# Two heads' scores on the two row halves of the array: three half-height passes in place of two full-height ones, in a fused attention, expert and feed-forward kernel

## The chip, the cores and the metric

One Trainium2 chip, one core. The metric is the time of one execution on the device in microseconds (us). PE is the matrix engine (TensorE), PEld its weight loads, DVE the vector engine, ACT the scalar engine, POOL GpSimd, SP the queue that issues most DMAs. PSUM is the memory into which PE writes; its pools here take it in banks.

## The reference

The program computes three stages one after another. Only the first matters for most of the change.

```
B, H, S, D = 2, 8, 768, 64                   # attention: 4 sink keys, a window of 128
scores = (q @ k.T) / sqrt(D); keep = (key < n_sink) | (0 <= row - key < window)
a = softmax(where(keep, scores, -1e9)); x = a @ v          # x becomes 1536 rows of 512
# experts: 8 of 512 -> 1024 -> 512 with relu, one for each row
logits = normalised(x) @ normalised(expert_emb).T / tau
y[row] = softmax(logits)[best] * relu(x[row] @ w1[best]) @ w2[best]
# feed-forward: 512 -> 2048 -> 512
out = leaky(y @ w_in) @ w_out
```

## The kernel before

**Attention.** Query rows are taken in blocks of 128, heads in groups of four. A step of the loop in `attention` is one block of one head: there are 2 batches x 2 groups x 6 blocks x 4 heads = 96 steps. At each step `score` makes one head's scores of a block against the keys that its window and the sinks can reach (256 or 288 columns). Some steps later `flip` turns the exponentials on PE, and `value` multiplies them with v (tiles `tp` and `xp`, lines L299, L317, L320). Beside these run, for the next group, the turning of q and k from rows to columns (`turns`, L206), and for each finished block of rows the router: its turn (L729) and its product with the expert embeddings (`lg`, L749).

**Two parts of each number.** Scores are products of numbers cast to `fp32r`. What the cast drops is kept too: q and k are held in a high part (the cast, written by ACT, L212 and L226) and a low part (the rest, written by DVE, L217 and L229). A head has 64 dimensions. Before, the tile `head_k` holds the high part of k on one half of the 128 partitions and the low part on the other, and `head_q` holds q's high part on both halves, and its low part on both. So one product over 128 rows gives q_high x (k_high + k_low), a second gives q_low x (k_high + k_low). For q to land on both halves it is copied on POOL before it is turned (L172), and each head's q is turned by itself. So a pair of heads takes 3 turns for k and 6 for q for each half of the rows.

**Order.** In the attention, a scheduler that simulates the engines sets the order of instructions on each engine; from the experts on, PE's order is that of the code. Each engine works through its own queue in order. Tiles in PSUM come from pools: `ps_sc` (scores, three banks, also the small router results `lg`, `rk`, `cnt`), `ps_t` (turned tiles, four banks), `ps_x` (one). A product into a tile waits until the earlier user of its buffer has been read. `stir` and `fill` are products whose results nobody reads.

**Behind the attention.** `rank_experts` and `route` find out on DVE which rows go to which expert, while PE works on one unit of a guessed expert (L1338, L1356). Then come the eight experts (`moe_wide`, `moe_narrow`, `moe_whole`) and the feed-forward part (`ffn`). Some weights are split into high and low parts in between (`Work.pop`, L1157 and L1158). `pick` checks that no score was out of the range in which the shortcut holds.

Of the kernel before, what the change touches and what calls it, by code (L numbers as in the profile page):

```python
# [57 lines left out]
TURNS = {(0, 0): ([0, 1, 2], [3, 4, 5, 6, 7, 8]), (0, 1): ([11, 13, 15, 17, 19, 21], [25, 26, 27, 28, 29, 30]),  # L58
         (1, 0): ([33, 35, 37, 39, 41, 43], [56, 57, 59, 60, 61, 62]), (1, 1): ([47, 49, 50, 51, 53, 54], [67, 69, 71, 73, 75, 77])}
# [89 lines left out]
def attention(c, ctx):  # L149
# [14 lines left out]
    def load_qk(b, pr, c0=0, n=QB):  # L164
        rk, rq = raws[b, pr] = c.raws[pr % 2]
        for j in range(2):
            nc.sync.dma_start(out=rk[:, c0:c0 + n, j, :],
                              in_=c.k[b, 2 * pr + j].rearrange("(c p) d -> p c d", p=P)[:, c0:c0 + n])
        for j in range(2):
            nc.sync.dma_start(out=rq[:, c0:c0 + n, j, 0, :],  # L170
                              in_=c.q[b, 2 * pr + j].rearrange("(c p) d -> p c d", p=P)[:, c0:c0 + n])
            c.copied = nc.gpsimd.tensor_copy(rq[:, c0:c0 + n, j, 1, :], rq[:, c0:c0 + n, j, 0, :])  # L172
# [22 lines left out]
    def turns(b, pr):  # L195

        rk, rq = raws[b, pr]
        own = slice(0, D), slice(D, P)  # L200
        two = [c.heads[(b * H + 2 * pr + j) % 8] for j in range(2)]
# [22 lines left out]
        def q_part(c0, j):  # L224
            t, w, qt = turn(rq[:, :, j], c0, f"q{j}"), slice(c0 * P, (c0 + 3) * P), two[j][1]
            nc.scalar.activation(out=qt[:, 0, w], in_=t, func=AF.Copy, scale=-0.125)  # L226

            def rest():
                c.low_half = nc.vector.scalar_tensor_tensor(out=qt[:, 1, w], in0=t, scalar=-0.125, in1=qt[:, 0, w].bitcast(F32),  # L229
                                                            op0=ALU.mult, op1=ALU.subtract)  # L230

            later(step[0] >= 0, rest)

        for j in range(2):
            heads[b, 2 * pr + j] = two[j]
        return [[lambda c0=c0, o=o: k_part(c0, o)] + [lambda c0=c0, j=j: q_part(c0, j) for j in range(2)]
                for c0, o in ((0, 0), (3, BEHIND))]

# [7 lines left out]
    copied = c.copied  # L246
# [18 lines left out]
    def score(b, g, i, h):  # L265
# [5 lines left out]
        off, n, m, _, s0 = SPAN[i]  # L271
        kt, qt = heads[b, 4 * g + h]
# [8 lines left out]
        c.scored = nc.vector.tensor_tensor_reduce(out=p, in0=sc[:, 0:n], in1=m, scale=1.0, scalar=3.0e38,  # L281
# [94 lines left out]
    for m in (2, 0, 2):  # L376
        turn[0, 0][0].pop(0)()
        stir(m)
    s = 0
    while s < n or after:  # L380
# [5 lines left out]
        if s < n:  # L386
# [17 lines left out]
            if s == 1:  # L404
                with tc.issue_after(copied.ins):
                    c.others()
# [13 lines left out]
def pick(c, T, over):  # L420
# [4 lines left out]
    part, big, ok = T([P, 1], "part"), T([P, 1], "big"), T([P, 4], "ok")  # L425
    nc.vector.tensor_reduce(out=part, in_=c.los, axis=AX.X, op=ALU.max)
# [315 lines left out]
def router_logits(c, t, pool=None):  # L742
# [3 lines left out]
    lp = (pool or c.psc).tile([P, E], F32, tag="sc", name=f"lg{c.uid()}")  # L746
    with c.tc.issue_after(turned.ins):
        for kk in range(4):
            c.logged = nc.tensor.matmul(lp, lhsT=xT[:, kk, :], rhs=c.embT[:, kk, :], start=(kk == 0), stop=(kk == 3))  # L749
    lg, top, idx, oh = c.lg[:, t, :], c.top[:, t], c.idx[:, t:t + 1], c.oh[:, t, :]  # L750
    nc.vector.tensor_scalar(out=lg, in0=lp, scalar1=0.0, scalar2=None, op0=ALU.add, op1=ALU.max, accum_out=top)
# [8 lines left out]
def router_rank(c, t0, t1, pool=None):  # L760
# [3 lines left out]
    rk = (pool or c.psc).tile([P, n, E], F32, tag="sc", name=f"rk{c.uid()}")  # L764
# [19 lines left out]
def choose(c):  # L784
# [5 lines left out]
    cp = c.psc.tile([P, E], F32, tag="sc", name="cnt0")  # L790
# [22 lines left out]
def choose_rows(c):  # L813
# [14 lines left out]
    ip = c.psc.tile([P, 1], F32, tag="sc", name="ip0")  # L828
# [45 lines left out]
def rank_experts(c, pool=None):  # L874
# [6 lines left out]
    cp = (pool or c.psc).tile([P, E], F32, tag="sc", name=f"cnt{c.uid()}")  # L881
# [40 lines left out]
def route(c, ctx):  # L922
# [45 lines left out]
    def rest():  # L968
# [65 lines left out]

        def chosen():
            with tc.issue_after(c.split.ins):
                pick(c, T, nov)

        return [chosen, place]
# [38 lines left out]
def slots(c):  # L1078
# [11 lines left out]
    for k in range(8):  # L1090
        o = end - (k + 1) * 4 * (KW + 2 * S)
        c.heads.append((c.nc.alloc_sbuf_tensor_at(f"head_k{k}", [P, KW], F32R, offset=o)[:],
                        c.nc.alloc_sbuf_tensor_at(f"head_q{k}", [P, 2, S], F32R, offset=o + 4 * KW)[:]))
    o = end - 8 * 4 * (KW + 2 * S) - 6 * QB * D * 8
    c.raws = [(c.nc.alloc_sbuf_tensor_at(f"raw_k{k}", [P, QB, 2, D], F32, offset=o + 3 * k * QB * D * 8)[:],
               c.nc.alloc_sbuf_tensor_at(f"raw_q{k}", [P, QB, 2, 2, D], F32, offset=o + (3 * k + 1) * QB * D * 8)[:])
# [185 lines left out]
def moe_wide(c, n, xT, gs, at, flow):  # L1282
# [5 lines left out]
    def up(f):  # L1288
# [151 lines left out]
def moe(c):  # L1440
# [46 lines left out]
    def tag(n):  # L1487
        return "xb" if n % 2 else "xa"

    every = [expert(n) for n in range(E)]  # L1490
    xT, todo = moe_x(c, BASE[0], WIDTH[0], tag(0), ORDER[0] in WHOLE)
# [80 lines left out]
def ffn(c):  # L1572
# [7 lines left out]
    for ch in range(nch):  # L1580
# [44 lines left out]
        for k in range(nt):  # L1625
# [78 lines left out]
```

## Time and profile before

| what | us |
|---|---|
| median of 3 runs (589.4 to 592.2) | 591.17 |
| the profiled execution | 592.47 |
| its span, from first to last instruction | 590.7 |
| PE busy / DVE / ACT / POOL | 580.3 / 373.6 / 277.4 / 65.6 |

The profiled execution lies 1.3 us above the median, and 1.8 us of its time lie outside the span. The attention takes the first 139 us, the experts follow up to about 320 us, the feed-forward part fills the rest. PE's matmuls overlap each other, so that a busy PE alone does not tell how fast it works; the chain of work that ended last gives the time that each group of products took from the end of the one before it.

### The profile page before, as it was taken

Reading aid. Unit: us, or ns where it says so; the run is one execution under the profiler, and the core shown is the slowest. Engines: PE = TensorE matmul, PEld = TensorE weight load, DVE = VectorE, ACT = ScalarE, POOL = GpSimd, SP = SyncE. Lnnn points to the kernel's source line nnn. Section 1 sums busy time; section 2 is a strip of 40 time slices with the busy share of each in tenths; the row PEclk is TensorE's granted clock in tenths of the full one; section 3 lists DMA queues with packets and bytes.
Section 4 is the critical chain, followed back from the end, with each engine's and each line's share of the span. In section 5 each row is a group of like instructions: output and inputs, shape, how many; then the busy total and the mean of one; then the engine's idle time right before and its main releaser. Section 6 shows DMA issues by size and latency. Waiting matters only on the chain.

```text
span 590.7 us, 9767 instructions
## 1 busy us (share of the span) xinstructions
PE 580.3 (98%) x3507; PEld 517.9 (88%) x3507; DVE 373.6 (63%) x903; ACT 277.4 (47%) x532; POOL 65.6 (11%) x195
## 2 busy tenths in 40 slices
PE   8999999999999999999999999999999999999995
PEld 4999999898999998899999888888888888888884
DVE  8999789665588956787991899954322223322230
ACT  4888788473494437743552544523322222322220
POOL 6223014111311000010000000001100001100001
PEclk9999999997999999999999999999999999999999
DMA  7656151191296459999977400000100000000001
GB/s 160 152 118 128 61 133 34 35 314 44 85 337 182 132 172 294 348 376 364 376 264 252 177 1 1 1 1 18 54 0 1 0 1 36 37 0 1 1 19 59
DMA packets 75178, 70.44 MB, mean 119 GB/s; under 512 B 41236, under 2 KB 57620, under 8 KB 75120
## 3 DMA queue, kind: packets, MB, share of 16 engines
q1 hardware_dynamic: 72736, 63.07, 34.2%
q0 software_dynamic: 2096, 6.64, 3.5%
q8 instruction: 30, 0.49, 0.3%
q14 instruction: 28, 0.23, 0.1%
q10 hardware_dynamic: 288, 0.00, 0.0%
HBM read 63.41 MB, written 6.29 MB: 118 GB/s over the span
## 4 chain that ended last, share of the span: by engine, by line
PE 94%; DVE 2%; issue 1%; ACT 1%; DMA 1%; DVEq 0%; POOL 0%; POOLq 0%; ACTq 0%
PE hp L1238 29%; PE acc L1238 28%; PE xp L317 6%; PE hp L1338 6%; PE acc L1356 6%; PE sc L276 4%; PE tp L299 3%; PE tq L206 2%; PE lg L749 2%; PE stir L362 2%; PE xp L320 1%; PE tr L1226 1%; PE tk L206 1%; PE xTp L729 1%; DVE slot L1158 1%
## 5 line engine op out<-in xcount | busy, mean ns | idle before, releaser
L1238 PE MATMUL acc<-slot,h 128*128 128x512 f32 x588 | 142.7, 390 | 0.0
L1238 PE MATMUL hp<-fxT,slot 128*128 128x512 f32 x576 | 137.1, 389 | 0.0
L1238 PEld LDWEIGHTS acc<-slot,h 128*128 128x128 f32 x588 | 109.6, 188 | 22.2
L1238 PEld LDWEIGHTS hp<-fxT,slot 128*128 128x128 f32 x576 | 108.1, 188 | 22.4
L1600 DVE TENSOR_TENSOR lk<-hp,lk 128x512 f32<-128x512 f32 x48 | 32.9, 689 | 97.2 <-ACT lk L1599 97.2
L1599 ACT ACTIVATE lk<-hp 128x512 f32<-128x512 f32 x48 | 28.5, 598 | 110.1 <-PE hp L1238 104.3
L285 ACT ACTIVATE p<-p,los 128x288 f32<-128x288 f32 (+2 forms) x96 | 45.3, 505 | 16.2 <-DVE los L281 15.7
L1158 DVE TENSOR_TENSOR slot<-slot_raw,slot 128x1024 fp32r<-128x1024 f32 x36 | 42.9, 1219 | 5.0 <-ACT slot L1157 5.0
L1634 POOL DMA_INDIRECT out_y<-y,sid x12 | 11.7, 975 | 304.2 <-DVE y L1633 282.6
L276 PE MATMUL sc<-head_k,head_q 128*128 128x288 f32 (+1 forms) x192 | 44.8, 329 | 0.6 <-DVE los L281 0.4
L317 PE MATMUL xp<-v,pt 128*128 128x65 f32 x352 | 43.7, 271 | 0.5 <-DVE x L331 0.5
L317 PEld LDWEIGHTS xp<-v,pt 128*128 128x128 f32 x352 | 42.2, 191 | 1.0 <-PE rk L766 0.6
L1602 DVE TENSOR_TENSOR h<-lk,h 128x512 fp32r<-128x512 f32 x43 | 29.5, 690 | 18.0 <-ACT h L1601 17.8
L1601 ACT CAST h<-lk 128x512 fp32r<-128x512 f32 x43 | 26.6, 620 | 29.2 <-DVE lk L1600 29.2
L1157 ACT CAST slot<-slot_raw 128x1024 fp32r<-128x1024 f32 x36 | 36.0, 1049 | 0.0
L1356 PE MATMUL acc<-h,slot_raw 128*128 128x184 f32 (+2 forms) x192 | 33.8, 320 | 0.1
L1238 PE MATMUL acc<-h,slot 128*128 128x352 f32 (+1 forms) x192 | 31.0, 309 | 0.7 <-DVE yT L1319 0.7
L276 PEld LDWEIGHTS sc<-head_k,head_q 128*128 128x128 f32 x192 | 28.8, 190 | 2.8 <-ACT head_q L226 0.6
L1356 PEld LDWEIGHTS acc<-h,slot_raw 128*128 128x128 f32 x192 | 30.7, 190 | 0.4 <-DVE yT L1362 0.4
L1238 PEld LDWEIGHTS acc<-h,slot 128*128 128x128 f32 x192 | 28.8, 188 | 0.9 <-DVE yT L1319 0.9
L299 PE MATMUL tp<-ident,p 128*128 128x128 f32 x176 | 29.2, 273 | 0.0
L1254 POOL DMA_INDIRECT rows<-xd,ids x15 | 16.2, 1080 | 113.8 <-PE tr L1226 102.1
(294 smaller groups left out, 912.3 us busy)
## 6 DMA issues: line engine op xcount, KB each, us to landing
slot_raw<-in_moe_w SPq DMA_DIRECT2D x48, 512.0 KB, 5.7
slot_first<-in_moe_w SPq DMA_DIRECT2D x16, 512.0 KB, 9.9
slot_wide<-in_moe_w_in SPq DMA_DIRECT2D x8, 1024.0 KB, 9.5
slot_wide<-in_moe_w_out SPq DMA_DIRECT2D x8, 1024.0 KB, 8.5
raw_k<-in_k SPq DMA_DIRECT2D x32, 96.0 KB, 2.5
raw_q<-in_q SPq DMA_DIRECT2D x32, 96.0 KB, 3.2
xd<-x SPq DMA_DIRECT2D x12, 256.0 KB, 2.1
v<-in_v SPq DMA_DIRECT2D x12, 192.0 KB, 3.5
```

The costliest lines, as they stand in the source:

```text
L276: nc.tensor.matmul(sc[:, 0:w], lhsT=qt[:, half, i * P:(i + 1) * P], rhs=kt[:, off:off + w], start=half == 0, stop=half == 1)
L285: c.raised = nc.scalar.activation(out=p, in_=p, func=AF.Exp, scale=-1.0, bias=lo)
L299: nc.tensor.transpose(u.t[:, h % 2, n, :], u.p[:, h, o:o + P], c.ident)
L317: nc.tensor.matmul(xp[:, h, :], lhsT=u.pt[h // 2][:, h % 2, n, :], rhs=vT[b, g][:, kb, h, :], start=h == 0 and n == 0, stop=h == 3 and i < ...
L1157: nc.scalar.copy(out=sl.g[0], in_=raw)
L1158: nc.vector.tensor_tensor(out=sl.g[1], in0=raw, in1=sl.g[0].bitcast(F32), op=ALU.subtract)
L1238: c.nc.tensor.matmul(out, lhsT=a[x], rhs=b[y], start=first and n == 0, stop=last and n == 2)
L1338: nc.tensor.matmul(hp, lhsT=g[:, kk, o:o + P], rhs=xT[:, 0, kk, :], start=kk == 0, stop=kk == 3)
L1356: nc.tensor.matmul(acc[k], lhsT=g[:, f % 2, k * P:(k + 1) * P], rhs=h, start=f == 0, stop=f == nf - 1)
L1599: nc.scalar.activation(out=raw, in_=hp, func=AF.Copy, scale=0.01)
L1600: nc.vector.tensor_tensor(out=raw, in0=hp, in1=raw, op=ALU.max)
L1602: y = nc.vector.tensor_tensor(out=h[:, 1, :], in0=raw, in1=h[:, 0, :].bitcast(F32), op=ALU.subtract)
```

## The change

A pair of heads now has one `head_k` (high and low part as two planes, each with head A on partitions 0 to 63 and head B on 64 to 127) and one `head_q` of the same shape. q is not copied, and q and k of a pair are turned together: 3 turns each for a half of the rows. ACT and DVE write all 128 partitions at once. At every second step `score` makes both heads' scores: three passes (low x high, high x low, high x high), each of two products over 64 rows, head A on the upper and head B on the lower half of the array, into two banks. PSUM is shared anew: two score tiles of two banks, three `ps_t` banks, which now also serve the router's small results. The table of steps at which turns are made (`TURNS`) is shorter.

Further edits: `lg` is computed 8 times side by side (64 columns in place of 8); the last block of rows of the output is scaled half by ACT and half by DVE; in `moe_wide`, for the second expert, one pop of weight splitting is moved a step later; the maximum over `los` in `pick` is a step of its own before it.

```
+LGW = 8
+PSC, PST = 2, 3
...
-    psc = ctx.enter_context(tc.tile_pool(name="ps_sc", bufs=3, space=PSUM))
+    psc = ctx.enter_context(tc.tile_pool(name="ps_sc", bufs=PSC, space=PSUM))
...
-    pst = c.pst = ctx.enter_context(tc.tile_pool(name="ps_t", bufs=4, space=PSUM))
+    pst = c.pst = ctx.enter_context(tc.tile_pool(name="ps_t", bufs=PST, space=PSUM))
...
-            c.copied = nc.gpsimd.tensor_copy(rq[:, c0:c0 + n, j, 1, :], rq[:, c0:c0 + n, j, 0, :])
...
         def k_part(c0, o):
             t, w = turn(rk, c0, "k"), slice(o, o + HALFK)
-            for j in range(2):
-                nc.scalar.copy(out=two[j][0][own[j], w], in_=t[own[j]])
+            nc.scalar.copy(out=kt[:, 0, w], in_=t)
 
             def rest():
-                for j in range(2):
-                    kt = two[j][0]
-                    nc.vector.tensor_tensor(out=kt[own[1 - j], w], in0=t[own[j]], in1=kt[own[j], w].bitcast(F32), op=ALU.subtract)
-                    if c0 == 0:
-                        for s0 in SNK:
-                            nc.gpsimd.tensor_copy(kt[:, s0:s0 + SINK], kt[:, 0:SINK])
+                nc.vector.tensor_tensor(out=kt[:, 1, w], in0=t, in1=kt[:, 0, w].bitcast(F32), op=ALU.subtract)
+                if c0 == 0:
+                    for s0 in SNK:
+                        nc.gpsimd.tensor_copy(kt[:, :, s0:s0 + SINK], kt[:, :, 0:SINK])
...
-        sc = psc.tile([P, W3], F32, tag="sc", name=f"sc{b}{g}{i}{h}")
-        w = max(n, 2 * P)
-        for half in range(2):
-            nc.tensor.matmul(sc[:, 0:w], lhsT=qt[:, half, i * P:(i + 1) * P], rhs=kt[:, off:off + w],
-                             start=half == 0, stop=half == 1)
+        if h % 2 == 0:
+            kt, qt = heads[b, 2 * g + h // 2]
+            u.sc = psc.tile([P, 2, 512], F32, tag="sc", name=f"sc{b}{g}{i}{h}")
+            w = max(n, 2 * P)
+            for k, (x, y) in enumerate(((1, 0), (0, 1), (0, 0))):
+                for j in range(2):
+                    own = slice(j * D, j * D + D)
+                    nc.tensor.matmul(u.sc[:, j, 0:w], lhsT=qt[own, x, i * P:(i + 1) * P], rhs=kt[own, y, off:off + w],
+                                     start=k == 0, stop=k == 2)
+        sc = u.sc[:, h % 2]
...
-    lp = (pool or c.psc).tile([P, E], F32, tag="sc", name=f"lg{c.uid()}")
+    lp = (pool or c.pst).tile([P, LGW, E], F32, tag="t", name=f"lg{c.uid()}")
...
-        c.work.pop((QX if f > 1 else 1) if n > 256 + 64 else QW, x, y)
         flow.later(LAGW, lambda: down(f, h))
+        if f == LAGW - 2 and gs is not c.gs_first:
+            flow.later(1, lambda: c.work.pop(QW, x, c.split))
+        else:
+            c.work.pop((QX if f > 1 else 1) if n > 256 + 64 else QW, x, y)
...
-            if k % 2:
-                nc.scalar.activation(out=y, in_=acc[k], func=AF.Copy, scale=c.sgate[:, t:t + 1])
-            else:
-                nc.vector.tensor_scalar(out=y, in0=acc[k], scalar1=c.sgate[:, t:t + 1], scalar2=None, op0=ALU.mult)
+            cut = DM // 2 if t == NTT - 1 else DM * (k % 2)
+            if cut:
+                nc.scalar.activation(out=y[:, 0:cut], in_=acc[k][:, 0:cut], func=AF.Copy, scale=c.sgate[:, t:t + 1])
+            if cut < DM:
+                nc.vector.tensor_scalar(out=y[:, cut:], in0=acc[k][:, cut:], scalar1=c.sgate[:, t:t + 1], scalar2=None, op0=ALU.mult)
```

PE's queue about a third into the attention, before: `sc` are scores, `xp` values, `tp` turned exponentials, `tk` and `tq` the turns of k and q, `sk` turned sinks. Each row is one group of products.

```order
L276 MATMUL sc_1149<-head_k_149,head_q_150 128x288 x2
L317 MATMUL xp_1133<-v_628,pt_997 128x65 x4
L317 MATMUL xp_1133<-v_628,pt_1017 128x65 x4
L276 MATMUL sc_1168<-head_k_151,head_q_152 128x288 x2
L276 MATMUL sc_1193<-head_k_145,head_q_146 128x288 x2
L307 MATMUL sk_1157<-ident,sp_1005 128x128
L206 MATMUL tk_1162<-ident,raw_k_155 128x128 x3
L299 MATMUL tp_1173<-ident,p_1010 128x128 x4
```

The same stretch of the queue after the change.

```order
L272 MATMUL sc_1095<-head_k_141,head_q_142 128x288
L296 MATMUL tp_1036<-ident,p_926 128x128 x4
L304 MATMUL sk_1066<-ident,sp_921 128x128
L272 MATMUL sc_1095<-head_k_141,head_q_142 128x288 x5
L206 MATMUL tk_1071<-ident,raw_k_147 128x128 x3
L272 MATMUL sc_1145<-head_k_143,head_q_144 128x288 x6
L314 MATMUL xp_1113<-v_574,pt_981 128x65 x4
```

Two products over 128 rows for each head have become six over 64 rows for each pair. They stand between products over 128 rows: the 288 score products of the attention form 49 unbroken runs in the whole queue after the change, mostly of six, six of them of twelve, some shorter; the first six runs, with seven pairs, stand among the `stir` products at the start or right behind them. Turns of q and k (L206) fall from 144 to 96, 18 to 12 of them for each pair of heads.

DVE's queue at the start of the attention, before, from the last mask to the first row of scores that is read (the row marked L281; `m` is a mask).

```order
L124 TENSOR_SCALAR m_215<-first 128x128
L217 TENSOR_TENSOR head_k_137<-tk_362,head_k_137 64x384
L217 TENSOR_TENSOR head_k_139<-tk_362,head_k_139 64x384
L229 SCALAR_TENSOR_TENSOR head_q_138<-tq_377,head_q_138 128x384
L229 SCALAR_TENSOR_TENSOR head_q_140<-tq_383,head_q_140 128x384
L217 TENSOR_TENSOR head_k_141<-tk_395,head_k_141 64x384
L217 TENSOR_TENSOR head_k_143<-tk_395,head_k_143 64x384
L229 SCALAR_TENSOR_TENSOR head_q_142<-tq_416,head_q_142 128x384
L281 ISA p_401,los<-sc_402,m_215 128x256
```

The same place after.

```order
L126 TENSOR_SCALAR m_203<-first 128x128
L214 TENSOR_TENSOR head_k_137<-tk_346,head_k_137 128x384
L226 SCALAR_TENSOR_TENSOR head_q_138<-tq_357,head_q_138 128x384
L214 TENSOR_TENSOR head_k_139<-tk_369,head_k_139 128x384
L226 SCALAR_TENSOR_TENSOR head_q_140<-tq_390,head_q_140 128x384
L278 ISA p_374,los<-sc_375,m_203 128x256
```

Seven operations ahead of the first scores have become four.

## Rows read from the trace of the kernel before

**Rows 1.** The page: the chain that ended last, share of the span by engine.

```profile
PE 94%; DVE 2%; issue 1%; ACT 1%; DMA 1%; DVEq 0%; POOL 0%; POOLq 0%; ACTq 0%
```

**Rows 2.** Chain in order of time, attention: start us, us taken, what, products.

```profile
36.92 0.48 PE sc L276 x4
...
99.16 0.54 PE sc L276 x4
99.70 0.44 PE tp L299 x4
100.35 1.74 PE xp L317 x16
...
102.69 0.33 PE tq L206 x3
103.02 0.79 PE lg L749 x8
```

**Rows 3.** PE's waits from 12 to 135 us: us in total, times, longest.

```profile
PE xp L317 <- DVE x L331: 0.5, 1, 0.5
PE sc L276 <- DVE los L281: 0.4, 1, 0.4
```

**Rows 4.** Groups by shape, first 150 us: busy us, mean ns; then idle before.

```profile
L276 PE MATMUL sc<-head_k,head_q 128*128 128x288 f32 x128 | 30.5, 334 | 0.4 <-DVE los L281 0.4
...
L217 DVE TENSOR_TENSOR head_k<-tk,head_k 64x384 fp32r<-64x384 f32 x32 | 17.7, 555 | 1.2 <-ACT head_k L212 0.3
```

**Rows 5.** Chain behind the 56-row transposes `tr` of the experts.

```profile
252.78 1.44 PE hp L1238 x12
...
255.83 0.38 PE tr L1226 x4
256.21 1.61 PE hp L1238 x12
```

**Rows 6.** Chain about the 72-row transposes of a later expert.

```profile
292.16 0.25 PE tr L1226 x4
292.41 1.19 PE hp L1338 x8
...
294.74 1.14 PE hp L1338 x8
```

**Rows 7.** Timeline of PE's weight loads, 255.6 to 256.1 us: start, us.

```profile
255.76 0.32 PEld L1226 LDWEIGHTS tr<-ident,rows 56*128 56x128 f32 x4 [0.17 <-issue]
```

**Rows 8.** Line L1226: times of one in ns (least, median, most), first and last start, shapes.

```profile
L1226 PEld LDWEIGHTS tr<-ident,rows x60: 133/140/144, 157.3 to 292.1; 128*128 128x128 f32 x40, 96*128 96x128 f32 x4, 32*128 32x128 f32 x4, 56*128 56x128 f32 x4
```

**Rows 9.** Timeline of DVE up to the first scores read.

```profile
7.80 1.14 DVE L217 TENSOR_TENSOR head_k<-tk,head_k 64x384 fp32r<-64x384 f32 x2
...
11.67 0.41 DVE L281 CUSTOM_DVE_ANT_0 p<-sc,m 128x256 f32<-128x256 f32 x1
```

**Rows 10.** Windows: length, busy us of each engine, PE's granted clock, DMA.

```profile
130.00:140.00 10.00, 10.00 (x83) 9.54 (x82) 5.67 (x33) 4.22 (x12) 1.09 (x2) 0.94 0.26 96
140.00:150.00 10.00, 9.70 (x71) 8.37 (x72) 4.79 (x30) 1.31 (x5) 0.50 (x1) 0.72 0.00 1
```

**Rows 11.** Chain between attention and experts.

```profile
139.27 1.51 PE lg L749 x8
...
141.65 1.91 PE hp L1338 x8
...
148.25 0.89 PE hp L1338 x8
```

**Rows 12.** Waits of the first 150 us: DVE's for the count of rows.

```profile
DVE key L884 <- PE rk L766: 1.9, 1, 1.9
```

**Rows 13.** PE's waits from 150 us on.

```profile
PE acc L1238 <- DVE yT L1319: 0.7, 1, 0.7
PE rows_ps L428 <- DVE ok L431: 0.4, 1, 0.4
```

**Rows 14.** Timeline of the last output row block.

```profile
584.43 0.69 ACT L1631 ACTIVATE y<-acc,sgate 128x512 f32<-128x512 f32 x1 [7.13 <-PE acc L1238]
```

More of the change, by code (lines that the diff above doesn't have):

```diff
@@ L199, in turns @@
         rk, rq = raws[b, pr]
-        own = slice(0, D), slice(D, P)
-        two = [c.heads[(b * H + 2 * pr + j) % 8] for j in range(2)]
+        kt, qt = heads[b, pr] = c.heads[(b * H // 2 + pr) % 4]
         def turn(src, c0, nm):
@@ L210, in k_part, with q_part @@
             t, w = turn(rk, c0, "k"), slice(o, o + HALFK)
-            for j in range(2):
-                nc.scalar.copy(out=two[j][0][own[j], w], in_=t[own[j]])
+            nc.scalar.copy(out=kt[:, 0, w], in_=t)
             def rest():
-                for j in range(2):
-                    kt = two[j][0]
-                    nc.vector.tensor_tensor(out=kt[own[1 - j], w], in0=t[own[j]], in1=kt[own[j], w].bitcast(F32), op=ALU.subtract)
-                    if c0 == 0:
-                        for s0 in SNK:
-                            nc.gpsimd.tensor_copy(kt[:, s0:s0 + SINK], kt[:, 0:SINK])
+                nc.vector.tensor_tensor(out=kt[:, 1, w], in0=t, in1=kt[:, 0, w].bitcast(F32), op=ALU.subtract)
+                if c0 == 0:
+                    for s0 in SNK:
+                        nc.gpsimd.tensor_copy(kt[:, :, s0:s0 + SINK], kt[:, :, 0:SINK])
             later(step[0] >= 0, rest)
-        def q_part(c0, j):
-            t, w, qt = turn(rq[:, :, j], c0, f"q{j}"), slice(c0 * P, (c0 + 3) * P), two[j][1]
+        def q_part(c0):
+            t, w = turn(rq, c0, "q"), slice(c0 * P, (c0 + 3) * P)
             nc.scalar.activation(out=qt[:, 0, w], in_=t, func=AF.Copy, scale=-0.125)
             def rest():
-                c.low_half = nc.vector.scalar_tensor_tensor(out=qt[:, 1, w], in0=t, scalar=-0.125, in1=qt[:, 0, w].bitcast(F32),
-                                                            op0=ALU.mult, op1=ALU.subtract)
+                nc.vector.scalar_tensor_tensor(out=qt[:, 1, w], in0=t, scalar=-0.125, in1=qt[:, 0, w].bitcast(F32),
+                                               op0=ALU.mult, op1=ALU.subtract)
             later(step[0] >= 0, rest)
[L234 to L237, printed above, removed]
+        return [[lambda c0=c0, o=o: k_part(c0, o), lambda c0=c0: q_part(c0)] for c0, o in ((0, 0), (3, BEHIND))]
     def group_turns(b, g):
@@ L375, in attention @@
     n = len(items)
-    for m in (2, 0, 2):
+    for m in (2, 2):
         turn[0, 0][0].pop(0)()
@@ L404, in attention @@
             if s == 1:
-                with tc.issue_after(copied.ins):
-                    c.others()
+                c.others()
         if 0 <= s - LAG1 < n:
@@ L417, in attention, with pick @@
     assert not any(x for t in turn.values() for x in t)
-def pick(c, T, over):
+def pick(c, T, over, part):
     nc = c.nc
-    part, big, ok = T([P, 1], "part"), T([P, 1], "big"), T([P, 4], "ok")
-    nc.vector.tensor_reduce(out=part, in_=c.los, axis=AX.X, op=ALU.max)
+    big, ok = T([P, 1], "big"), T([P, 4], "ok")
     rows = c.ptr.tile([P, P], F32, tag="tr", name="rows_ps")
@@ L763, in router_rank @@
     n = t1 - t0
-    rk = (pool or c.psc).tile([P, n, E], F32, tag="sc", name=f"rk{c.uid()}")
+    rk = (pool or c.pst).tile([P, n, E], F32, tag="t", name=f"rk{c.uid()}")
     for lhs, rhs, first in ((c.tri, c.oh[:, t0:t1], True), (c.ones, c.cum[:, t0:t1], False)):
@@ L789, in choose @@
     io8 = c.iota[:, 0:E]
-    cp = c.psc.tile([P, E], F32, tag="sc", name="cnt0")
+    cp = c.pst.tile([P, E], F32, tag="t", name="cnt0")
     nc.tensor.matmul(cp, lhsT=c.ones, rhs=c.cum[:, T0, :], start=True, stop=True)
@@ L827, in choose_rows @@
     V.scalar_tensor_tensor(out=c.mine, in0=c.rq[:, 0:T0], scalar=0.0, in1=has, op0=ALU.is_equal, op1=ALU.mult)
-    ip = c.psc.tile([P, 1], F32, tag="sc", name="ip0")
+    ip = c.pst.tile([P, 1], F32, tag="t", name="ip0")
     for t in range(T0):
@@ L880, in rank_experts @@
     ioe = c.iota[:, 0:E].rearrange("p (o e) -> p o e", o=1)
-    cp = (pool or c.psc).tile([P, E], F32, tag="sc", name=f"cnt{c.uid()}")
+    cp = (pool or c.pst).tile([P, E], F32, tag="t", name=f"cnt{c.uid()}")
     nc.tensor.matmul(cp, lhsT=c.ones, rhs=c.cum[:, NTT - 1, :], start=True, stop=False)
@@ L1033, in place, with highest @@
             V.tensor_tensor(out=c.sgate, in0=lst[:, 2, :], in1=lst[:, 3, :], op=ALU.add)
+        part = T([P, 1], "part")
+        def highest():
+            with tc.issue_after(c.split.ins):
+                V.tensor_reduce(out=part, in_=c.los, axis=AX.X, op=ALU.max)
         def chosen():
             with tc.issue_after(c.split.ins):
-                pick(c, T, nov)
-        return [chosen, place]
+                pick(c, T, nov, part)
+        return [highest, chosen, place]
     def hot(row128, dt):
@@ L1089, in slots @@
     end, c.heads = at + (NSL - 2) * 8192, []
[L1090 to L1096, printed above, removed]
+    for k in range(4):
+        o = end - (k + 1) * 8 * (KW + S)
+        c.heads.append((c.nc.alloc_sbuf_tensor_at(f"head_k{k}", [P, 2, KW], F32R, offset=o)[:],
+                        c.nc.alloc_sbuf_tensor_at(f"head_q{k}", [P, 2, S], F32R, offset=o + 8 * KW)[:]))
+    o = end - 4 * 8 * (KW + S) - 4 * QB * D * 8
+    c.raws = [(c.nc.alloc_sbuf_tensor_at(f"raw_k{k}", [P, QB, 2, D], F32, offset=o + 2 * k * QB * D * 8)[:],
+               c.nc.alloc_sbuf_tensor_at(f"raw_q{k}", [P, QB, 2, D], F32, offset=o + (2 * k + 1) * QB * D * 8)[:])
               for k in range(2)]
@@ L1490, in moe @@
     every = [expert(n) for n in range(E)]
+    c.gs_first = every[0]
     xT, todo = moe_x(c, BASE[0], WIDTH[0], tag(0), ORDER[0] in WHOLE)
```

17 lines of the change are left out of this document (8 added, 9 removed).

## The prediction

> **What bounds the kernel now.** I read the page first, then the chain in order of time, then PE's waits. The chain that ended last lies on PE for 94% [rows 1], so the questions are whether PE's queue has any slack in the attention, and what each product costs there. In the chain, groups of products follow each other without a break [rows 2]: 4 scores of 288 columns in 0.54 us (0.135 each), 4 of 256 in 0.48 (0.12), 4 transposes in 0.44 (0.109), 16 values in 1.74 (0.109), 8 router products in 0.79 (0.099). A mean duration of 334 ns [rows 4] is a latency; the pace is 0.135. PE's whole waiting in the attention is 0.9 us [rows 3]. So in the attention PE's queue is full, and what it saves or pays there moves the end by as much. DVE and ACT, though much work leaves them, gain nothing by themselves, since PE hardly waits for them. The exception is the start: the first scores are read at 11.67 us, behind seven DVE operations that run back to back from 7.80 [rows 9].
>
> **The change, part by part** (us; minus is a gain).
>
> *Turns.* 48 of 144 products of 0.11 go [rows 2]. 12 belong to the first group, turned while PE still does idle `stir` products, so 36 x 0.109 = -3.9.
>
> *Scores, streaming.* A pair of heads took four full-height products, 4 x 0.135 or 4 x 0.12. If both halves of the array really stream at once, it takes three: -0.13 a pair. Of 48 pairs 7 stand in the start, so 41 x 0.13 = -5.3.
>
> *Scores, change of height.* So far all scores are products over 128 rows. The trace shows products over few rows mainly in the experts. Around the 56-row transposes [rows 5] the four transposes take 0.38, and the 12 products behind them 1.61, where the 12 of one step earlier took 1.44. The 72-row ones [rows 6] take 0.25, and the products behind them 1.19 where the next took 1.14: nearly nothing. Both are short operands, but only 56 rows fit a half of the array. So going to half height and back costs (0.38 - 0.25) + (1.61 - 1.44) = 0.30, as I read it because the array empties at each change and the next weight load is then laid bare. A transpose's load is short; in this sort of row they start 0.06 apart ((0.32 - 0.14) / 3, 0.14 being the length of one [rows 7, 8]). A score's load is longer: values with 65 columns and router products with 8 both stand 0.10 to 0.11 apart [rows 2], so the load sets that pace. That adds 0.05 on the way in: 0.35 a run. The queue after the change has 49 runs, 43 of them behind the start: +15.1. Bounds: nothing, if loads of scores can go ahead of the change of height, and 0.45, if both of the two long loads are laid bare.
>
> *Scores, the second half's lag.* Head B's load follows A's. By the row, loads start 0.06 apart [rows 7], and B ends so much after A: 43 x 0.06 = +2.6. The Trainium skill (TensorE: Matmul & The Clock Gate, Part 3: Packing small matmuls) says that products on different row groups start some 4 ns apart, so that a set takes one product's time plus about 4 ns for each further one. By that the lag would be 0.2 in all and the sum 2.4 lower; no row here shows it, and I keep the row's.
>
> *Start.* Four DVE operations of 0.55 [rows 4] stand ahead of the first scores in place of seven: -1.6. POOL's copies of q (32 of them) also go; they lie before the turns, within this term. Bounds: 0, if the last q lands late, and -3, since the second half of the first group saves as much again before PE is full.
>
> *Clock.* The granted clock is 0.94 and 0.72 in the two windows from 130 to 150 us [rows 10]: at half level (1.2 GHz) for (0.06 + 0.28) x 10 / 0.5 = 6.8 us. It falls after a stretch with router products of 8 columns among transposes. There 8 router products take 1.51, 8 expert products 1.91, against 0.89 later [rows 11]. DVE waits 1.9 for the row counts, which stand behind these products in PE's queue [rows 12]. With 64 columns the products may keep the clock up; then the counts come about 0.6 + 1.0 earlier (1.51 and 1.91 less 0.89), and the following half-speed products shrink too. I take -2.0, between 0 and -3.4 (half of 6.8). The wider products cost 96 x (0.108 - 0.099) [rows 2] = +0.9.
>
> *Second expert.* PE waits 0.7 and 0.4 there [rows 13], at the places of the moved pop and of `pick`: -1.0, between 0 and -1.1. *Last rows.* Half of 0.69 [rows 14] on each engine: -0.3.
>
> *PSUM.* Three banks for turned tiles in place of four, with the router's small tiles among them. Today no wait of PE on such a bank is in its list [rows 3], and DVE, which empties them, has 17 us less to do (16 + 16 operations of 0.55 [rows 4]). I take 0, up to +7 (rival below).
>
> *Sum:* -3.9 - 5.3 + 15.1 + 2.6 - 1.6 - 2.0 + 0.9 - 1.0 - 0.3 = +4.5. On the profiled execution's 592.5 that is 597.0; it lies 1.3 above the median of the runs, so on the median **595.7 us**, 0.8% slower. Less than 0.5% either way (588.2 to 594.1) is about what this kernel's runs can't tell from no change.
>
> **The rivals.**
>
> *1. The change of height is nearly free for scores: faster.* Place: each of the 43 runs. The price of 0.30 is from four transposes, not from the 32-bit products of the scores; if the half-height loads slip in while the last full-height product streams, 0.1 a run is left, and B's lag goes too. 4.5 - 43 x 0.25 - 2.6 = -8.9: 582.3. Without the lag, it decides at 0.31 a run: the other terms sum to -13.2, which is 43 x 0.31; at 0.24 the time is 0.5% faster. For it: 0.30 comes from one place, and DVE and ACT leave PE freer. Against: the 56 rows and the 72 rows differ by little else, and both ends of the gap show.
>
> *2. The weight loads of the halves go one after the other.* Each pass then needs two loads of 0.108, more than the 0.135 that it streams: six loads 0.65 plus 0.35, or 1.00 a run in place of 0.39 + 0.06 + 0.35 = 0.80: +8.6, 604. With the products one after another too, 6 x 0.13 + 0.35 = 1.13: +14, 610. The Trainium skill (TensorE: Matmul & The Clock Gate, LDWEIGHTS) says that a load's time goes by its columns, not its rows, so that a half-height one saves nothing. The Trainium skill (TensorEngine Tiling (Array Packing), Key Properties) says that different tiles can load and multiply in parallel. By the one without the other, 604; by both, the forecast. No run here shows which. For it: the pace of 0.10 to 0.11 of narrow products shows a load-bound PE. Against: the halves have their own rows.
>
> *3. PE waits for PSUM.* Three banks hold the turns until DVE has made the low part, a step later. If one block of each group in two (12 of 24) waits once for an emptying of 0.6, +7: 602. Against: today's 0.9 us of waits, none of it on a turned tile.
>
> **How the numbers follow.** Forecast (price 0.25 to 0.40, loads side by side; 591 to 600) 0.43, of which 0.14 below 594.1; rival 1 (579 to 590) 0.38, of which 0.03 above 588.2; rival 2 0.13; rival 3 0.06. So faster 0.35, same 0.14 + 0.03 = 0.17, slower 0.29 + 0.13 + 0.06 = 0.48. The range runs from 582 to 605: it leaves out about 0.1 of rival 1's low end and 0.05 to 0.1 of rival 2's high end. The forecast's own range is 591 to 600.
>
> **What would show it.** In the profile after: a run of six scores takes 0.75 to 0.85 us in the chain from the end of the full-height product before it to the end of that behind it, beyond what these take elsewhere, with no load of scores starting until 0.2 after the last full-height product; about 0.5 to 0.6 would be rival 1, 1.0 and more rival 2. The two heads' products of a pass start at almost the same time in the forecast, 0.1 apart in rival 2. The first scores are read at about 10 us. The granted clock stays at 1.0 between 130 and 150 us. PE's list of waits stays near 1 us in the attention; several us there on `tp`, `tk` or `tq` would be rival 3. The attention's last turn of rows (L729) ends about 8 us later than now, if the sum up to there is right (-3.9 - 5.3 + 15.1 + 2.6 - 1.6 + 0.9 = +7.8). Most likely to make it wrong: the price of 0.35 a run, since 43 runs multiply it.

## The result and the profile after

The changed kernel takes 598.05 us (median of 4 runs, 597.37 to 598.42), the kernel before beside it 590.42 (4 runs). The ratio is 1.0121, 95% interval 1.0095 to 1.0147: 1.2% slower. The profiled execution took 597.37, its span 595.6 (before 590.7).

The chain in order of time, after: start us, us taken, what, products. It answers to [rows 2].

```profile
67.70 0.11 PE sk L304
67.81 0.59 PE sc L272 x6
68.41 0.48 PE tk L206 x3
...
71.94 0.33 PE tq L206 x3
...
72.48 0.84 PE lg L744 x8
...
112.06 0.44 PE xp L317 x2
...
113.78 0.98 PE sc L272 x12
114.76 1.93 PE xp L314 x16
```

Read a run of scores together with the group behind it, whose first weight load is late. Three turns take 0.48 behind a run and 0.33 elsewhere, so six scores of a pair cost 0.59 + 0.15 = **0.74 us**, where the two heads took 0.54 before. The run of twelve costs 0.98 + (1.93 - 1.74 [rows 2]) = 1.17: 0.43 for three further passes, about the 0.135 of each that they stream. Three passes of 0.135 leave 0.34 of the 0.74 for the change of height and back.

The other runs bear this out. Of the 43 runs behind the start, the first 40 hold one to twelve products each; the last three stand among the waits at the end. Take the time from the end of the full-height product before a run to the end of the one behind it, less 0.109 for that one and 0.12 or 0.135 for each pass begun. What is left is 0.32 to 0.35 us in every run, 0.336 in the mean, and the same in a second execution. A product without its partner takes a whole pass, as two runs of 256 columns show, the first of two products and the second of one; ten of the 43 runs hold an odd number.

```profile
75.55 0.31 PE sc L272 x2
...
104.36 0.31 PE sc L272
```

The timeline of the same place, PE and then PE's weight loads.

```profile
67.54 0.28 PE L304 MATMUL sk<-ident,sp 128*128 128x128 f32 x1
67.74 0.66 PE L272 MATMUL sc<-head_k,head_q 64*128 64x288 f32 x6
68.34 0.55 PE L206 MATMUL tk<-ident,raw_k 128*128 128x128 f32 x3
...
67.43 0.20 PEld L304 LDWEIGHTS sk<-ident,sp 128*128 128x128 f32 x1
67.74 0.43 PEld L272 LDWEIGHTS sc<-head_k,head_q 64*128 64x128 f32 x6
68.33 0.31 PEld L206 LDWEIGHTS tk<-ident,raw_k 128*128 128x128 f32 x3 [0.17 <-issue]
```

The first score's load starts only 0.20 after the start of the last full-height product, at the same time as its own product, while the load of `sk`, among full-height work, runs 0.11 ahead of its product; on the way out the weight loads stand still for 0.17 before the first full-height one.

PE's waits from 100 to 150 us, after.

```profile
PE sc L272 <- DVE los L278: 1.1, 2, 0.6
PE xTp L724 <- DVE x L328: 1.0, 1, 1.0
PE lg L744 <- ACT xT L727: 0.9, 2, 0.7
```

And the windows of the last 37.7 us of the attention, after (length, busy us of PE, PEld, DVE, ACT, POOL, granted clock, DMA).

```profile
120.00:130.00 10.00, 8.37 (x63) 7.18 (x63) 5.69 (x39) 4.80 (x13) 3.35 (x5) 0.83 0.59 198
130.00:140.00 10.00, 8.80 (x76) 8.24 (x74) 3.86 (x15) 2.97 (x8) 0.00 (x0) 1.00 0.79 276
...
sum 37.70, PE 33.56 PEld 29.18 DVE 21.00 ACT 16.53 POOL 5.26; mean PE 8.39 PEld 7.30 DVE 5.25 ACT 4.13 POOL 1.32
```

PE stands idle 37.70 - 33.56 = 4.1 us there, and between 120 and 130 us the clock is at half (1.2 GHz) for 0.17 x 10 / 0.5 = 3.4 us, behind the two waits of `sc` (120.1 and 121.4 us). The start of the last turn of rows closes the attention (all instructions of line L724: ns of one, first and last start).

```profile
L724 PE MATMUL xTp<-ident,x x48: 271/273/330, 56.0 to 147.6; 128*128 128x128 f32 x48
```

The chain at the first experts and behind them, the first scores that DVE reads, and the last output rows (timelines of ACT and of DVE), after.

```profile
166.97 1.15 PE hp L1240 x7
...
327.96 2.08 PE hp L1240 x9
```

```profile
9.84 0.41 DVE L278 CUSTOM_DVE_ANT_0 p<-sc,m 128x256 f32<-128x256 f32 x1
...
589.16 0.47 ACT L1638 ACTIVATE y<-acc,sgate 128x256 f32<-128x256 f32 x1 [7.41 <-PE acc L1240]
...
589.66 0.48 DVE L1640 TENSOR_SCALAR y<-acc,sgate 128x256 f32<-128x256 f32 x1 [3.83 <-ACT y L1638]
```

The two halves of the last block run one after the other: DVE waits for ACT's part of `y`, and 0.69 [rows 14] has become 0.98.

### The profile page after: what moved, and what is told of

It is laid out like the page before. It is cut to its first block, busy times and chain, and to the rows that moved or that the text cites. A ratio compares the mean times of both kernels' runs of the same rounds, so it can differ in the third digit from the quotient of the medians.

```text
span 595.6 us, 9690 instructions
## 1 busy us (share of the span) xinstructions
PE 582.8 (98%) x3555; PEld 506.4 (85%) x3555; DVE 359.1 (60%) x872; ACT 262.3 (44%) x500; POOL 52.3 (9%) x147
## 4 chain that ended last, share of the span: by engine, by line
PE 95%; DVE 2%; ACT 1%; issue 1%; DMA 1%; SPq 0%; POOL 0%; DVEq 0%; POOLq 0%; ACTq 0%
PE hp L1240 29%; PE acc L1240 29%; PE xp L314 6%; PE hp L1343 6%; PE acc L1361 6%; PE sc L272 4%; PE tp L296 4%; PE lg L744 2%; PE xp L317 1%; PE tr L1228 1%; PE tk L206 1%; PE xTp L724 1%; PE tq L206 1%; PE stir L359 1%; DMA raw_q<-in_q 1%
## 5 line engine op out<-in xcount | busy, mean ns | idle before, releaser
L282 ACT ACTIVATE p<-p,los 128x288 f32<-128x288 f32 (+2 forms) x96 | 43.5, 503 | 12.4 <-DVE los L278 11.5
L272 PE MATMUL sc<-head_k,head_q 64*128 64x288 f32 (+1 forms) x288 | 32.2, 322 | 1.1 <-DVE los L278 1.1
L272 PEld LDWEIGHTS sc<-head_k,head_q 64*128 64x128 f32 x288 | 21.2, 184 | 10.2 <-issue 5.2
```

Source lines behind the costliest of these rows:

```text
L272: nc.tensor.matmul(u.sc[:, j, 0:w], lhsT=qt[own, x, i * P:(i + 1) * P], rhs=kt[own, y, off:off + w], start=k == 0, stop=k == 2)
L282: c.raised = nc.scalar.activation(out=p, in_=p, func=AF.Exp, scale=-1.0, bias=lo)
```

## The experiments

Theory: each change of height and back costs about 0.35 us; 43 of them behind the start outweigh what the change saves. Rivals: the loss comes from waits and the clock at the end of the attention; or from the new sharing of PSUM. Each kernel was timed beside the kernel before, at 589.2 to 589.5 us.

**A price for the change of height alone.** Two kernels with the same order of operations on every engine: R is 128 in the first and 64 in the second.

```
+        if h % 2 == 0:
+            nc.tensor.matmul(sc[:, W3:], lhsT=qt[0:R, 0, i * P:(i + 1) * P], rhs=kt[0:R, off:off + 64], start=True, stop=True)
```

> The kernel before, with 48 further products of 64 columns whose results nobody reads, each over all 128 rows, one at every second step of the attention ahead of that step's scores, into spare columns of the score tile. It is the measure for the next kernel, which has the same queue on every engine. Both theories: each product adds about its load's 0.11 us behind the start (some 41 of them), so 4 to 5 us more than before, 595.

> The same 48 further products at the same places, but over 64 rows: each is a run at half height of its own between products over 128 rows. Theory (a change of height and back costs about 0.35 us whatever is computed there): about 41 x 0.35 = 14 us above the kernel with products over 128 rows, less the part in which the queue has slack: 10 to 15 us. Rival (the price is not the height but the splitting in three passes and the waits of the new order): within 2 us of it.

Measured: 594.52 over 128 rows (ratio 1.0089, 1.0073 to 1.0106), 606.41 over 64 rows (1.0303, 1.0286 to 1.0320). One place in the chain, first over 128 rows, then over 64 (L276 is the added product).

```profile
67.71 0.13 PE sc L276
67.84 0.32 PE sc L278 x2
```

```profile
66.50 0.22 PE sc L276
66.72 0.47 PE sc L278 x2
```

The product and the scores behind it take 0.69 in place of 0.45. In all, 11.9 us for 41 products is 0.29 each, in a kernel that has none of the other edits. The height has a price of its own, near the 0.30 read from four transposes [rows 5 to 8], and it is not a matter of three passes or of order.

**Height taken out of the changed kernel.**

```
-            for k, (x, y) in enumerate(((1, 0), (0, 1), (0, 0))):
-                for j in range(2):
+            for j, x, y, one, end in ((1, 0, 0, True, True), (0, 1, 0, True, False), (0, 0, 0, False, True)):
...
-                    nc.tensor.matmul(u.sc[:, j, 0:w], lhsT=qt[own, x, ...], rhs=kt[own, y, off:off + w], ...)
+                nc.tensor.matmul(u.sc[:, j, 0:w], lhsT=qt[:, x, ...], rhs=kt[:, y, off:off + w], ...)
```

> The changed kernel with each pair's scores made of three products over all 128 rows in place of six over 64: the same streaming (3 x 0.12 to 0.135), no change of height. What it leaves out: the two heads' products are not kept apart, so both heads get the sum of the two heads' scores, and the low part of k is left out; all that follows is done as before. The scheduler orders a little differently (47 runs of scores). Theory (0.355 us for each change of height and back): 43 x 0.355 = 15 us less up to the end of the attention, if PE stays fed; with some of it lost to waits 10 to 15: 583 to 588. Rival (the loss is from the order, the waits and the clock at the end of the attention, not from the height): within 4 us of the changed kernel.

Measured: the sums of two heads' scores left the range of the shortcut, and the program went its long way behind the feed-forward part (3486 us), so only the attention of this run is read. Its last turn of rows, and the sum of the windows from 100 to 137.5 us.

```profile
L722 PE MATMUL xTp<-ident,x x48: 270/272/328, 51.2 to 137.4; 128*128 128x128 f32 x48
```

```profile
sum 37.50, PE 33.26 PEld 29.62 DVE 19.56 ACT 15.32 POOL 4.95; mean PE 8.31 PEld 7.41 DVE 4.89 ACT 3.83 POOL 1.24
```

The attention ends 10.2 us earlier than in the changed kernel, at the low end of what the theory gave and 4.4 less than 43 x 0.34. Some 1.7 of that (an estimate) is the clock, at half for 6.8 us here (granted 0.66 from 110 to 120 us) where it was 3.4; the rest was not separated. PE's idle time at the end is still 4.2 us. So height and idle time are two causes, and the second doesn't follow from the first.

**Fewer runs.** All four heads' scores at once, `PSC` = 1 with tiles of four banks.

> The changed kernel with all four heads' scores of a block made at once, in one score tile of four banks where there were two of two: 36 unbroken runs in place of 49, the same products. Theory (0.355 us for each run): 13 x 0.355 = 4.6 us less than the changed kernel, 593.5, if the single score tile brings no waits. Rival (the cost lies in the streaming of six passes, or at the end of the attention): no gain, 598, or a loss of some us from waits for the score tile, which then show as waits of sc.

Measured: 595.72 (1.0099, 1.0066 to 1.0132). The interval overlaps that of the changed kernel, though the four runs (592.6 to 596.8) all lie below that kernel's six (597.0 to 598.9). The chain shows what was gained and lost.

```profile
63.80 0.91 PE sc L273 x12
64.70 1.03 PE lg L745 x8
...
108.48 0.44 PE xp L318 x2
...
114.65 0.46 DVE p L279
...
118.48 2.73 PE xp L315 x16
```

Twelve scores of 256 columns cost 0.91 + (1.03 - 0.84) = 1.10, against 2 x 0.74: in the changed kernel a run of six at this width, with the same group behind it, takes 0.55 + (1.03 - 0.84). At 108.48 the kernel stands 3.6 us ahead of the same product in the changed kernel (112.06), with 14 runs fewer by then; a wait of 1.1 us for a load of k early in the attention took part of it. Then PE waits some 4 us for DVE, the clock is at half for twice as long, and 1.1 us of lead is left at the last turn of rows. Fewer runs are worth their price; the end of the attention took it back.

**Scores held back.**

```
+                    with tc.issue_after(c.flipped.ins) if c.flipped else nullcontext():
```

> The changed kernel with each pair's scores held behind the last turning of exponentials that was recorded before them, so that scores cannot run far ahead of the turnings; 54 runs in place of 49. Rival to the theory of the height (much of the loss comes from scores that run ahead, so that PE stands idle some 4 us in the last 30 us of the attention, where it stood idle 0.9 before): 3 to 4 us less than the changed kernel, 594 to 595, with PE's idle time at the attention's end back at about 1 us. Theory of the height alone: 5 more runs cost 1.8 us, 600.

Measured: 600.98 (1.0181, 1.0147 to 1.0215). The chain at the end of the attention.

```profile
116.82 0.18 DVE chkey L795
...
120.57 3.43 PE xp L316 x15
```

The wait stays: PE still comes to the choice of the guessed expert on DVE (`choose`, 116.8 to 120.5) with nothing else to do. In the last 37.7 us of its attention PE stands idle 3.2 us, though only 64 products stand in its queue between the last score and the last turn of rows, where the changed kernel has 120 and the kernel before 55. The clock is at half for some 10 us there (granted 0.52 from 120 to 130 us). As a test of height against waits the edit doesn't decide; it does say that keeping the scores from running ahead is not enough to fill the wait.

**The sharing of PSUM, added to before and taken from after.** First the kernel before with tiles of two banks for two heads' full-height scores, three `ps_t` banks, `lg`, `rk` and `cnt` among them.

```
-        sc = psc.tile([P, W3], F32, tag="sc", name=f"sc{b}{g}{i}{h}")
+        if h % 2 == 0:
+            u.sc = psc.tile([P, 2, 512], F32, tag="sc", name=f"sc{b}{g}{i}{h}")
...
+            for j in range(2):
+                kt, qt = heads[b, 4 * g + h + j]
```

> The kernel before, whose scores stay products over 128 rows, with the new sharing of PSUM alone: two heads' scores are made at every second step into one of two score tiles of two banks, three banks for turned tiles and the router's small results. One turn of q in the start is made earlier. In PE's queue 120 products now stand between the last score and the attention's last turn of rows, as in the changed kernel, where before it were 55. Theory (the new sharing lets the scores run ahead, and the end of the attention is left with too little for PE): some 4 us of idle time of PE in the last 30 us of the attention, a fall of the clock there, 3 to 6 us more than before, 593 to 595. Rival (this idle time comes with the change of height or with cheaper scores): within 1.5 us of before.

Measured: 603.79 (1.0243, 1.0197 to 1.0289), more than expected. Its last turn of rows, the sum of the windows from 112 to 149.7 us, and PE's waits from 20 to 100 us.

```profile
L732 PE MATMUL xTp<-ident,x x48: 270/273/421, 60.0 to 149.6; 128*128 128x128 f32 x48
```

```profile
sum 37.70, PE 33.75 PEld 30.60 DVE 20.92 ACT 15.90 POOL 5.27; mean PE 8.44 PEld 7.65 DVE 5.23 ACT 3.97 POOL 1.32
```

```profile
PE sc L278 <- DVE head_k L217: 0.7, 1, 0.7
PE sk L310 <- ACT pt L305: 0.7, 1, 0.7
PE lg L752 <- DVE head_k L217: 0.5, 1, 0.5
```

PE stands idle 4.0 us at the end here too, without a single change of height. Besides, PE now waits some 3 us in the middle, for turned tiles to be emptied and in the first line for the low part of k itself; the changed kernel with its fewer turns doesn't (its list from 20 to 100 us is empty). The clock falls for 10 us from 147 us on. The idle time at the end and in the middle is about 6 of the 11.3 us by which the last turn of rows comes later than in the kernel before (138.3, below); the rest, with what the turn made earlier adds in the start, was not separated.

Then the changed kernel with three score banks and four `ps_t` banks, as before.

```
-            u.sc = psc.tile([P, 2, 512], F32, tag="sc", name=f"sc{b}{g}{i}{h}")
+            u.sc = [psc.tile([P, W3], F32, tag="sc", name=f"sc{b}{g}{i}{h + j}") for j in range(2)]
```

> The changed kernel with the old sharing of PSUM: three score tiles of one bank, of which a pair takes two, four banks for turned tiles, the router's small results among the scores. 47 products stand behind the last score. The scores now form 73 unbroken runs in place of 49. Theory (0.355 us for each run, and the waits at the end of the attention come from the sharing): 24 x 0.355 = 8.5 us more, less about 4 for the idle time at the end: 602 to 603, with PE idle for less than 2 us in the last 30 us of the attention. Rival (the sharing has no part in the waits): 606 to 607 with the same idle time. If runs cost nothing: 594.

Measured: 606.60 (1.0282, 1.0258 to 1.0305). The sum of the windows from 120 to 157.2 us, where the last turn of rows stands, and two runs in the chain.

```profile
sum 37.20, PE 36.56 PEld 31.29 DVE 21.57 ACT 17.32 POOL 3.66; mean PE 9.14 PEld 7.82 DVE 5.39 ACT 4.33 POOL 0.91
```

```profile
54.71 0.59 PE sc L272 x3
...
58.79 0.60 PE sc L272 x6
```

The idle time at the end is gone (0.6 us), so it belongs to the sharing, and with it the fall of the clock is gone. The time is the rival's figure, but for a reason that my expectation left out. Many pairs fell apart: one head's three products stand alone, and take 0.59 where two heads' six take 0.60. Each pair that is split pays the whole run twice, 0.74, not only a change of height. Behind the start the runs of scores take 15 us more than in the changed kernel; less the idle time (3.5) and the fall (1.7) that are gone, that fits the last turn of rows, which comes 9.5 later (157.1). The same rows show that the second half of the array costs nothing beside the first. The Trainium skill (TensorE: Matmul & The Clock Gate, Part 3: Packing small matmuls) has products on different row groups start about 4 ns apart; these rows agree, to their 0.01.

**The further edits.** First the kernel before with the wide `lg`, the moved pop and the step for the maximum alone; then that with the cut of the last rows.

```
+LGW = 8
...
-        c.work.pop((QX if f > 1 else 1) if n > 256 + 64 else QW, x, y)
+        if f == LAGW - 2 and gs is not c.gs_first:
+            flow.later(1, lambda: c.work.pop(QW, x, c.split))
```

> The kernel before with three of the further edits alone: lg computed 8 times side by side, the moved pop of the second expert, the maximum over los in a step of its own. Scores, turns and PSUM as before. Theory (the small edits are worth what the prediction gave them): -2.0 for the clock, +0.9 for the wider products, -1.0 for the second expert: 2 us less than before, 0.4%; the granted clock then stays at 1.0 at the end of the attention, where it fell for 6.8 us. Rival (the clock falls because PE stands idle, whatever the width of lg): the fall stays, and the time is within 1 us of before.

> The kernel before with the same three edits and the last block of output rows scaled half by ACT, half by DVE. Against the kernel without this cut: by the prediction 0.3 us less; by the profile of the changed kernel, where the two halves took 0.47 and 0.48 one behind the other in place of one of 0.69, 0.3 us more. It is to be read from the last rows of the profile; the times differ too little.

Measured: 587.58 (0.9955, 0.9936 to 0.9974) and 588.02 (0.9959, 0.9940 to 0.9978). The first is the fastest kernel of this study, 0.45% under before and under the changed one by more. Its chain at the last turn of rows, the first expert and behind the experts, and the last rows of the second.

```profile
138.11 0.39 PE xTp L729 x2
...
157.41 0.67 PE hp L1245 x4
...
318.38 3.67 PE hp L1245 x16
```

```profile
579.82 0.47 ACT L1643 ACTIVATE y<-acc,sgate 128x256 f32<-128x256 f32 x1 [7.13 <-PE acc L1245]
580.33 0.48 DVE L1645 TENSOR_SCALAR y<-acc,sgate 128x256 f32<-128x256 f32 x1 [3.83 <-ACT y L1643]
```

Against the kernel before in its execution without a fall of the clock (below) the experts end 1.7 earlier, and the rest is as it was: in the medians the gain of 2 us is the second expert's, both waits gone, not the clock's. The clock shows in how the runs spread. Of the 19 runs of the kernel before beside these two, 13 took 588.8 to 589.8 us at a mean granted clock of 0.996 to 0.999, and six took 591.7 to 592.8 at 0.993, as the profiled execution of [rows 10] did. All 20 runs of the two kernels lie within 587.0 to 588.4, at 0.996 to 0.999. By chance alone that would come less than once in a hundred times, so the small edits most likely keep the fall away; that it is the wide `lg` among them, as the prediction had it, was not separated. The cut costs 0.3: again the halves run in turn. The times of the two can't tell that; the rows do.

**The clock.** The changed kernel with `LGW = 1`, and both kernels once more.

> The changed kernel with lg computed once (8 columns) as before, nothing else. Theory of the prediction (the narrow router products bring the clock down): the clock falls for about 6.8 us in place of 3.4 at the end of the attention, +1.7, and the narrower products give back 0.9: some 1 us more than the changed kernel. Rival (the clock falls behind a stretch in which PE stands idle): the fall is the same to one step, and the time 0 to 1 us less.

> The kernel before once more, unchanged. Its profiled execution took 592.47 us and had the clock at half for 6.8 us behind the attention; the two kernels with products added to it have the same narrow router products there and show no fall at all. If the fall comes and goes between executions: no fall or another length, and a span shorter by about half of what is missing, 587 to 588 without a fall; then the clock term of the prediction belongs to that one execution and not to the median. If the narrow products bring it down each time: 6.8 us again, a span of 590 to 591.

> The changed kernel once more, unchanged. Its fall stood at 124.4 us for 3.4 us, behind a stretch in which PE waited for DVE. If it follows from that stretch: a fall at 120 to 125 us again, one or two steps of 3.4 us long; PE's waits at the end of the attention as before, and a span of 594 to 598.

Measured: 599.46 (1.0167, 1.0117 to 1.0217), 589.49 (0.9998) and 597.95 (1.0125). The kernel before, again: its last turn of rows, the chain at the first experts and behind them, and two windows.

```profile
L729 PE MATMUL xTp<-ident,x x48: 272/273/329, 54.1 to 138.3; 128*128 128x128 f32 x48
```

```profile
138.11 0.44 PE xTp L729 x2
...
157.45 0.68 PE hp L1238 x4
...
320.11 2.06 PE hp L1238 x9
```

```profile
130.00:140.00 10.00, 10.00 (x86) 9.36 (x85) 5.83 (x35) 4.37 (x12) 1.24 (x2) 1.00 0.25 94
140.00:150.00 10.00, 9.69 (x95) 9.23 (x93) 6.87 (x36) 2.42 (x7) 2.23 (x3) 1.00 0.06 11
```

The same program, with the same eight narrow products, and no fall: 0.94 and 0.72 in [rows 10] belong to one execution. Its span is 587.6 in place of 590.7, and the time between the last turn of rows and the first expert is 3 us shorter. Its runs lie between 589.0 and 593.0, which fits a fall that costs 3 us and comes in some executions; in which, and why, stays open. The changed kernel shows 0.83 from 120 to 130 us both times. With the narrow `lg` it is 0.66 (6.8 us at half in place of 3.4) and the time 1.4 us more, with intervals that overlap: the figures of the theory, but in one profile, and the kernel with four heads at once and the one with full-height passes also show 6.8 us with the wide `lg`. That the fall there comes from PE's waits is supported by its absence in the changed kernel with the old sharing, not proved.

## Why the prediction was right, and where it was not

The direction and the mechanism held, the sum fell short: +4.5 forecast, 595.7; measured +7.6, 598.05. The prediction gave "slower" no more than 0.48, so the direction was a near call. That it came within 2.4 us is in part luck: the lag that isn't there (2.6 too much) stood against the new idle time and the clock (3.2 and 3.7 too little). Between the span of before without a fall of the clock (587.6) and that of the changed kernel (595.6, its own fall included) the change costs 8.0. Up to the last turn of rows it is +9.3 (138.3 to 147.6) where the sum had +7.8; from there to the first expert +0.2; the experts -1.7; the rest +0.2.

| term | forecast | found | from |
|---|---|---|---|
| turns | -3.9 | -3.9 | 36 fewer, 0.33 for three still |
| streaming | -5.3 | -5.3 | 0.12 or 0.135 a pass fits runs of one to twelve |
| change of height | +15.1 | +14.6 | 43 x 0.34; 0.32 to 0.35 in 40 runs |
| second half's lag | +2.6 | 0 | three products 0.59, six 0.60 |
| start | -1.6 | -1.8 | first scores read at 9.84, were at 11.67 [rows 9] |
| wider lg | +0.9 | 0 at the end | last turn at 138.11 with and without, though eight products took 0.84, were 0.79 |
| PSUM | 0 | +3.2 | idle at the end 4.1, was 0.9 [rows 3] |
| clock | -2.0 | +1.7, and 0 behind | half of 3.4 us at half level, an estimate |
| second expert | -1.0 | -1.7 | both waits of [rows 13] gone |
| last rows | -0.3 | +0.3 | the halves run in turn |

The found terms add up to 7.1; 0.9 of the 8.0 is left, nearly all of it in the attention. The ten odd products, which take a whole pass where half a pass was counted, would be some 0.6 of it (an estimate, 10 x 0.065).

**The change of height** was the term that decided, and its price of 0.35, worked out from four transposes and the values behind them [rows 5 to 8], was right to 0.01 in the runs of 32-bit scores. That it was so close is in part luck: the prediction's own bounds were nothing and 0.45, and 0.30 came from a single place. That there is such a price, paid once for each run, is shown by adding it to the kernel before and by taking it out of the changed one. Both marks were there: no load of scores until 0.20 after the last full-height product, and a run at 0.74, just under the 0.75 to 0.85 that was named, since the lag isn't there. Rival 1 (0.1 a run) and rival 2 (loads one after the other, 1.0 a run) are both out. The Trainium skill (TensorEngine Tiling (Array Packing), Key Properties) says that changing the tiling mode drains TensorE, without a price; here it is 0.34 us for both ways.

**The second half's lag** failed: "By the row, loads start 0.06 apart" took the pace among four loads to the same rows of the array for that between its two halves. Three products on one half take as long as six on both, so the rows leave nothing for a lag.

**PSUM** failed: "Today no wait of PE on such a bank is in its list" was true, and the changed kernel has hardly any on a turned tile either (0.4 us). But the new sharing brings the idle time at the end, with the change of height and without it, and the old sharing takes it away: 4.1 us where the sign named was "near 1 us". PE reaches the choice of the guessed expert with too little of its own left. Rival 3 named the right edit with the wrong place and mechanism. By what path the sharing does it is not shown. Scores do run further ahead with it (120 products between the last score and the last turn of rows, where 55 stood), but the kernel that holds them back (64) still stands idle 3.2 us.

**The clock** failed twice: the fall in the profile of before comes in about a third of its executions (six of 19), so the median has little of it to give back, and a new fall came at 124 us, where that one stood at 139. The forecast also corrected the same thing twice, since the 1.3 us by which that execution lay above the median was part of this fall. The thought behind the term was not refuted: with the small edits alone the fall stayed away in all 20 runs. **The last rows** failed because the two halves were taken to run side by side. The row names ACT's `y` as what DVE waited for: this is an order that the program sets between two writers of one tile, and the runs don't show what the engines could do without it.

Without the new waits and the fall (3.2 + 1.7) the changed kernel would by this estimate stand at about 593, still slower than before: the 12.7 that turns, streaming, start and second expert give back don't reach the price of 43 changes of height. The part worth keeping is the small edits without the cut of the last rows.

## What to carry to other kernels

Half-height products in a queue of full-height ones are priced by the run, not by the product: count the unbroken runs, multiply by 0.34 us, and set against it what the packing saves (here 0.13 a pair). By this estimate it pays from about three pairs to a run; no run here had more than two. Keep partners together, since an odd product takes a whole pass. A new sharing of PSUM is a new order of work: look for new waits wherever PE depends on another engine's chain, as at the end here. Before a term is put on a stretch at half clock, look at a second execution and at the granted clock of every timed run.

## What was not expected of the hardware

- One head's three products over 64 rows take as long alone (0.59) as two heads' six on both halves (0.60), and a change to 64 rows and back costs 0.32 to 0.35 us however many products the run holds.
- An added 64-column product costs 0.13 us over 128 rows (5.4 us for 41) and 0.29 more over 64.
- The same program had its clock at half for 6.8 us in one profiled execution and not at all at that place in another, 3.1 us of span apart; six of 19 timed runs look like the first, and none of 20 with the small edits.
